# Attention and a two-layer network on one core: zero products ahead of the first chunk, another order of the first loads, and chunk 1's preparation between ticks

## The chip, the cores and the metric

The kernel runs on one core of a Trainium2 chip. A core has a matrix engine (TensorE, PE in the profile, with its weight loads shown as PEld), a vector engine (VectorE, DVE), a scalar engine (ScalarE, ACT), a general engine (GpSimd, POOL) and a synchronising engine (SyncE, SP). Each runs its own instructions in program order. Sixteen DMA engines move data between HBM and the on-chip memory (SBUF); the accumulation memory (PSUM) has eight banks, which PE writes and DVE and ACT read. The metric is the device time of one execution in microseconds, the median of several runs.

## The reference

For 4 batches, 8 heads, 768 tokens and head size 64 it computes causal attention. Heads 0, 2 and 6 see all earlier tokens. The other five heads see the first 4 tokens ("sinks") and the last 64. The output of all heads is put side by side (3072 tokens of 512 numbers) and goes through two products with a leaky ReLU between:

```
scores = scale * (q @ k.T), masked        # mask by head: causal, or causal and (sink or window)
x = softmax(scores) @ v                   # (4, 8, 768, 64) -> (3072, 512)
h = x @ w_in                              # (3072, 512) @ (512, 2048)
out = max(0.01 * h, h) @ w_out            # (3072, 2048) @ (2048, 512)
```

## The kernel before

**Tiling.** The 3072 tokens are cut into 8 chunks of 384: chunk n is half c = n % 2 of batch n // 2. For a chunk four stages follow one another: preparation (q and k transposed, so that the head dimension lies on the partitions), attention, product 1 and product 2. Heads go in pairs: pair p holds heads 2p and 2p+1.

**Stages as lists of functions.** The order of all instructions is written out by hand. A stage is a list of small functions ("slots"), and `merge` (L489 and on) deals one list evenly between the elements of another.

- `prep_first` (L227) prepares chunk 0: PE transposes k and q into PSUM, DVE and ACT copy them to SBUF.
- `prep_pair` (L193 to L214) prepares one pair of chunk 1 or 2: six PE transposes (three of k, then three of q, each of 128 tokens) into one PSUM bank, two DVE copies of k (L206) and, by ACT, one copy of q (L208).
- `prep_dma` (L216) prepares the later chunks with six transposing DMAs from SP's queue (L223 and L225); `v_shift` (L172) moves v by 64 tokens with two DMAs.
- `Attention.slots`: slot t computes the scores of unit t on PE and their exponential on ACT (L334, L370, and L312 for the sinks), DVE applies a mask where one is needed, and the product with v of unit t-LAG follows (L296). A full head has two units in an even chunk and five in an odd one, a window head has one, and the sinks of all heads are one. After a pair's last unit `finish` (L390 and on) divides by the sums on DVE (`linv` L400, `xs` L402), and three slots later `x_t` transposes the result back on PE (L411) and ACT copies it to `xt` (L412).
- `in_slots` (product 1): 16 ticks of four matmuls, 384 columns each (L457), each followed by ACT's leaky ReLU into `g` (L459). Ticks 4i to 4i+3 use quarter i of `w_in`.
- `out_slots` (product 2): three tiles of 128 tokens, 16 matmuls of 512 columns each (L470), cut into parts of 2 to 4 matmuls. After a tile's last part DVE copies it out of PSUM (L475), and SP stores it.

**PSUM.** The banks are named by tag: `ph`, `psS` and `po` have two each, `py` and `pt` one each. A new use of a tag waits until the last reader of the bank before it is done. Ticks 0 to 11 of chunk 0's product 1 take `ph` and `psS` in turn; chunk 1's scores take `psS`; the preparation of chunk 1 takes `py` and `pt` in turn.

**Loads.** Nearly all loads are issued by POOL, each as three or six pieces or one, and they pass through one software DMA queue in the order of their issue. Eight of its DMAs can be under way: each waits for the one eight places before it. The order at the start is: q of chunk 0, the identity, v of chunk 0 (`va`, three pieces; `vb`, two), all masks (`masks`, L142 to L151), quarters 0 to 2 of `w_in`, then k, q and v of chunk 1, quarter 3 of `w_in`, `w_out`, chunk 2. k of chunk 0 comes by SP's queue.

**Order around the change (L507 to L561).** Loads and constants, `prep_first`, attention of chunk 0 (`a0`, with LAG 4), ticks 0 to 11 of chunk 0's product 1 (`in0`), then the four pairs of chunk 1 in the order 0, 1, 3, 2 with the first three slots of its attention (`a1`) between them, slots 3 to 7, the last four ticks dealt among slots 8 to 15, and the first eight parts of product 2 (`out0`) dealt among the other slots of `a1`. From chunk 2 on a loop overlaps product 1 of chunk n, product 2 of chunk n-1 and attention of chunk n+1.

Of the kernel before, what the change touches and what calls it, by code (L numbers as in the profile page):

```python
# [11 lines left out]
FP32 = mybir.dt.float32  # L12
# [5 lines left out]
CH = 384  # L18
# [3 lines left out]
def kernel(  # L22
# [12 lines left out]
    nc = tc.nc  # L35
# [106 lines left out]
    def masks():  # L142
        nc.gpsimd.memset(m_caus[:], 1.0)
        keep(m_caus[:], [[1, 128]], ALU.is_ge, 0, -1)
        nc.gpsimd.memset(m_w[:], 1.0)
# [70 lines left out]
    def prep_dma(n):  # L216
        b, c = divmod(n, 2)
        i = b % 2
        qts[n] = rot.tile([128, 4, CH], BF16, name="qt", tag="qt", bufs=2)
        for g in range(3):  # L220
            t = slice(128 * g, 128 * g + 128)
            tk = slice(CH * c + 128 * g, CH * c + 128 * g + 128)
            nc.sync.dma_start_transpose(out=kt[i].rearrange("p a e t -> p (a e) t")[:, :, tk],  # L223
                                        in_=kz[n % 2][:, g].rearrange("p h d -> p (h d)"))
            nc.sync.dma_start_transpose(out=qts[n][:, :, t], in_=cast["q", n][:, g].rearrange("p h d -> p (h d)"))  # L225

    def prep_first():  # L227
# [48 lines left out]
    class Attention:  # L276
# [131 lines left out]
        def x_t(self, p, xs, tag="pt"):  # L408
            pt = bank(tag, [128, 2, 4, 128], BF16)
            for j in range(3):  # L410
                nc.tensor.transpose(pt[:, 0, j, :], xs[:, j], ident[:])  # L411
            nc.scalar.activation(out=xts[self.n][:, p, :], in_=pt[:, 0, 0:3, :], func=ACTF.Copy)  # L412
# [95 lines left out]
    make_identity(nc, ident)  # L508
    nc.vector.memset(sv[:], 0.0)
# [17 lines left out]
    for i in range(4):  # L527
# [3 lines left out]
                   x_tags=("pt", "ph", "psS", "pt")).slots(order=[0, 2, 1, 3, 4, 5, 6, 7], LAG=4, XLAG=3, sink_after={0, 2})  # L531
    run(a0[0:4])
# [35 lines left out]
    for n in range(2, NCH):  # L568
# [3 lines left out]
        if n + 2 < NCH:  # L572
            prep_dma(n + 2)
            v_shift(n + 2, nc.sync)
# [47 lines left out]
```

The softmax here doesn't subtract the row's maximum and nothing guards it: scores larger than these inputs give would overflow.

## Time and profile before

| what | value |
|---|---|
| median of 6 runs | 246.38 us (244.63 to 246.98) |
| the profiled execution's own time | 245.31 us |
| its span, first to last instruction | 243.6 us |
| PE busy | 224.5 us, 92% |
| ACT busy | 131.9 us, 54% |
| DVE busy | 90.3 us, 37% |
| POOL busy | 80.3 us, 33% |
| read from HBM, written | 27.81 MB, 6.29 MB |
| share of the closing chain: PE, DMA, DVE, ACT, POOL | 72%, 13%, 5%, 3%, 3% |

A row of a timeline gives start, duration, engine, line, operation, output and inputs with their shape, how often it stands in a row, and in brackets the engine's idle time just before it with what ended that. Ends of matmuls are modelled and stand some 0.2 us behind the last column, so the distance between starts tells the pace. A row of stretches gives, for each engine, the busy time and the number of instructions, then the clock that the throttle granted, the load of the DMA engines and GB/s. The clock column reads 1.00 also where the trace has no record of it: the first record begins 15.6 us into the span.

### The profile page before, as it was taken

The page shows a single profiled execution, that of the slowest core. Times are in us where ns is not written, and L with a number is a line of the kernel's source. Part 1 is how long each engine was busy: PE and PEld are TensorE (multiplying, and loading weights), DVE is VectorE, ACT ScalarE, POOL GpSimd, SP SyncE. Part 2 cuts the span into 40 slices and gives each one's busy share as a digit, 9 for nine tenths or more (in the row PEclk, how much of TensorE's full clock was granted, in tenths as well). Part 3 has the DMA queues.
Part 4 walks back from the last instruction along what each step waited for, and adds up shares of the span by engine and source line. Part 5 has one row for each costly group of instructions (what it writes and reads, how often), then busy time and mean ns, then how long its engine had stood idle before and what let it go on. Part 6 is the DMA issues. An engine that isn't in the chain of part 4 may idle for free.

```text
span 243.6 us, 4966 instructions
## 1 busy us (share of the span) xinstructions
PE 224.5 (92%) x1957; PEld 137.0 (56%) x1984; DVE 90.3 (37%) x257; ACT 131.9 (54%) x284; POOL 80.3 (33%) x108
## 2 busy tenths in 40 slices
PE   1788879899999999799999999999999999999994
PEld 0475546556665577465655666566556665555553
DVE  6787332706545234324421343234411342111121
ACT  2585688434663598656536665456446764333300
POOL 8994742679309961496260000000000000000000
PEclk9999999999999999999999999999999999999999
DMA  8999999999999999999999921477210111111012
GB/s 159 143 153 182 163 236 205 159 180 152 130 177 217 182 169 115 183 168 169 173 180 169 194 57 59 82 119 180 78 58 4 61 35 59 43 43 46 39 47 86
DMA packets 114858, 30.78 MB, mean 126 GB/s; under 512 B 105620, under 2 KB 110996, under 8 KB 114836
## 3 DMA queue, kind: packets, MB, share of 16 engines
q0 software_dynamic: 78304, 13.51, 77.9%
q1 hardware_dynamic: 36432, 16.95, 34.6%
q8 instruction: 15, 0.25, 0.4%
q14 instruction: 7, 0.06, 0.1%
q10 hardware_dynamic: 100, 0.02, 0.1%
HBM read 27.81 MB, written 6.29 MB: 140 GB/s over the span
## 4 chain that ended last, share of the span: by engine, by line
PE 72%; DMA 13%; DVE 5%; ACT 3%; POOL 3%; issue 1%; SPq 1%; ACTq 0%
PE ph L457 26%; PE py L470 19%; PE pt L470 6%; PE po L296 5%; PE psS L329 5%; DMA qb<-in_q_dram 4%; PE psS L470 4%; DMA qt<-qb 3%; DMA xt<-xs 3%; PE psS L365 2%; DMA f<-in_k_dram 2%; POOL kz L86 2%; DVE o L475 2%; PE psS L457 2%; PE ph L470 1%
## 5 line engine op out<-in xcount | busy, mean ns | idle before, releaser
L457 PE MATMUL ph<-xt,w_in_bf 128*128 128x384 bf16 x488 | 99.2, 326 | 0.2
L459 ACT ACTIVATE g<-ph 128x384 bf16<-128x384 f32 x122 | 60.0, 492 | 57.3 <-PE ph L457 56.6
L470 PE MATMUL py<-w_out_bf,g 128*128 128x512 bf16 (+1 forms) x238 | 63.0, 372 | 1.5
L457 PEld LDWEIGHTS <-w_in_bf 128*128 128x128 bf16 x512 | 46.0, 97 | 29.9 <-issue 0.3
L470 PEld LDWEIGHTS <-g 128*128 128x128 bf16 x400 | 36.0, 97 | 28.4 <-issue 1.4
L334 ACT ACTIVATE at<-psS 128x384 bf16<-128x384 f32 x81 | 38.8, 491 | 13.4 <-PE psS L329 11.6
L329 PE MATMUL psS<-qt,kt 128*128 128x384 bf16 (+2 forms) x104 | 26.6, 296 | 3.3 <-ACT at L334 1.2
L93 POOL DMA_DIRECT2D qb<-in_q_dram x24 | 21.4, 912 | 21.9 <-DMA qt<-qb 9.9
L475 DVE COPY o<-py 128x512 f32<-128x512 f32 (+1 forms) x16 | 10.8, 674 | 45.3 <-PE py L470 45.3
L86 POOL DMA_DIRECT2D kz<-in_k_dram x30 | 22.5, 777 | 14.7 <-DMA kt<-kz 12.8
L93 POOL DMA_DIRECT2D va<-in_v_dram x24 | 21.3, 914 | 6.6 <-DMA w_out_bf<-in_moe_w_out_dram 3.3
L370 ACT ACTIVATE ats<-psS 128x384 bf16<-128x384 f32 x38 | 18.5, 492 | 4.9 <-PE psS L365 4.4
L296 PE MATMUL po<-va,at 128*128 128x65 bf16 x237 | 20.4, 196 | 0.3 <-DVE at L338 0.3
L296 PEld LDWEIGHTS <-at 128*128 128x128 bf16 x252 | 16.4, 100 | 7.6 <-DVE at L338 1.2
L402 DVE TENSOR_TENSOR xs<-po,linv 128x384 bf16<-128x384 f32 x30 | 16.7, 557 | 1.0
L329 PEld LDWEIGHTS <-kt 128*128 128x128 bf16 x108 | 10.7, 101 | 10.5 <-issue 3.3
L340 DVE TENSOR_TENSOR at<-at,m_caus 128x128 bf16<-128x128 bf16 x24 | 5.4, 224 | 30.2 <-ACT at L334 30.1
L470 PE MATMUL pt<-w_out_bf,g 128*128 128x512 bf16 x57 | 15.7, 379 | 0.4
L365 PEld LDWEIGHTS <-kt 128*128 128x128 bf16 x240 | 12.4, 101 | 5.2 <-issue 0.2
L296 PEld LDWEIGHTS <-ats 128*128 128x128 bf16 x240 | 11.9, 99 | 3.8 <-DVE xs L402 0.3
L365 PE MATMUL psS<-qt,kt 128*128 128x64 bf16 x228 | 13.1, 195 | 0.0
L338 DVE TENSOR_TENSOR at<-at,m_caus 128x256 bf16<-128x256 bf16 x24 | 7.0, 292 | 15.8 <-ACT at L334 15.5
(102 smaller groups left out, 189.3 us busy)
## 6 DMA issues: line engine op xcount, KB each, us to landing
out_dram<-o SPq DMA_DIRECT2D x23, 256.0 KB, 3.0
qb<-in_q_dram POOLq DMA_DIRECT2D x24, 128.0 KB, 6.3
va<-in_v_dram POOLq DMA_DIRECT2D x24, 128.0 KB, 7.3
w_in_bf<-in_moe_w_in_dram POOLq DMA_DIRECT2D x4, 512.0 KB, 7.7
w_out_bf<-in_moe_w_out_dram POOLq DMA_DIRECT2D x4, 512.0 KB, 13.7
kz<-in_k_dram POOLq DMA_DIRECT2D x30, 64.0 KB, 6.5
vb<-va SPq DMA_DIRECT2D x8, 195.0 KB, 7.4
vb<-va SPq DMA_DIRECT2D x6, 130.0 KB, 5.0
```

The costliest lines, as they stand in the source:

```text
L86: nc.gpsimd.dma_start(out=kz[n % 2][:, g, hh::2, D * hh : D * hh + D], in_=nat[nm][b, c, :, hh::2, g])
L93: nc.gpsimd.dma_start(out=o, in_=nat[nm][b, c, :, :, g])
L296: nc.tensor.matmul(o, lhsT=lhsT, rhs=rhs, start=first, stop=False, skip_group_check=True)
L329: nc.tensor.matmul(s[:, off : off + w], lhsT=kt[i][:, p, hh, 128 * kj : 128 * kj + 128], rhs=qts[n][:, p, lo:CH], start=(j == 0), stop=(j ...
L334: nc.scalar.activation(out=a[:, 0:off], in_=s[:, 0:off], func=ACTF.Exp, scale=SM)
L365: nc.tensor.matmul(s[:, 64 * m : 64 * m + 64], lhsT=kt[i][:, p, hh, k0 : k0 + 128], rhs=qts[n][:, p, 64 * m : 64 * m + 64], start=(m == 0) ...
L370: nc.scalar.activation(out=av_, in_=s[:, 0:CH].rearrange("p (j e f) -> p j e f", j=3, e=2), func=ACTF.Exp, scale=SM)
L402: nc.vector.tensor_tensor(xs[:], po[:, :, :, 0:D], linv.to_broadcast([128, 3, 2, D]), op=ALU.mult)
L457: nc.tensor.matmul(ph[:, 0:CH], lhsT=w_in_bf[:, g, 128 * t : 128 * t + 128], rhs=xts[n][:, g, :], start=(g == 0), stop=(g == KG - 1))
L459: nc.scalar.activation(out=gs[n][:, t, :], in_=ph[:, 0:CH], func=ACTF.Prelu, alpha=0.01)
L470: nc.tensor.matmul(py[n][:, 0 : c1 - c0], lhsT=gs[n][:, ng, 128 * tt : 128 * tt + 128], rhs=w_out_bf[:, ng, c0:c1], start=(ng == 0), stop= ...
L475: nc.vector.tensor_copy(o[:, 0 : c1 - c0], py[n][:, 0 : c1 - c0])
```

## The change

Five edits, all at or before the start of chunk 2:

1. `warm_up(n, w)` issues n matmuls of zeros, w columns wide, into a `psS` bank that nothing reads. It is called with 9 of 512 columns at the start, with 9 of 128 ahead of the second half of k in `prep_first`, with 8 ahead of q's first piece and 2 ahead of each later one, and with 12 ahead of chunk 0's attention. Its first call puts a memset of 128x512 on DVE. In chunk 0, `x_t` issues 6, 4, 6 and 10 transposes of the identity (by pair) ahead of its own three.
2. `masks` is cut in two. The causal mask (`mask_causal`) now stands ahead of v's loads on POOL, the other two masks stand between quarter 0 and quarter 1 of `w_in`.
3. Nine ticks of product 1 stand ahead of chunk 1's preparation, not twelve; ticks 9, 10 and 11 follow its first, second and third pair.
4. The list of slots that is dealt among the first eight parts of product 2 has six empty slots at its end, not four.
5. `prep_dma` returns its seven steps as a list, which its callers run at once; the steps and their order are the same.

```diff
-    def masks():
+    def mask_causal():
         nc.gpsimd.memset(m_caus[:], 1.0)
         keep(m_caus[:], [[1, 128]], ALU.is_ge, 0, -1)
+
+    def masks():
         nc.gpsimd.memset(m_w[:], 1.0)
...
+    idle = {}
+
+    def warm_up(n, w=128):
+        if not idle:
+            idle["s"] = bf("idle", 512)
+            nc.vector.memset(idle["s"][:], 0.0)
+            idle["d"] = bank("psS", [128, 512], FP32)
+        for _ in range(n):
+            nc.tensor.matmul(idle["d"][:, 0:w], lhsT=idle["s"][:, 0:128], rhs=idle["s"][:, 0:w], start=True, stop=True)
...
             if nm == "q":
                 continue
+            if half == 1:
+                warm_up(9)
             for e in range(2):
...
+        warm_up(8)
         for g in range(3):
+            warm_up(2 if g else 0)
             for p in range(4):
...
         def x_t(self, p, xs, tag="pt"):
             pt = bank(tag, [128, 2, 4, 128], BF16)
+            for j in range((6, 4, 6, 10)[p] if self.n == 0 else 0):
+                nc.tensor.transpose(pt[:, 1, j % 4, :], ident[:], ident[:])
             for j in range(3):
...
     load(0, "q")
     make_identity(nc, ident)
+    warm_up(9, 512)
     nc.vector.memset(sv[:], 0.0)
...
+    mask_causal()
     load(0, "v")
     load_vb0()
+    load_w("in", 0)
     masks()
-    for i in range(3):
-        load_w("in", i)
+    load_w("in", 1)
+    load_w("in", 2)
     load(1)
...
+    warm_up(12)
     run(a0[0:4])
...
-    run(in0[0:12])
+    run(in0[0:9])
 
     for j, p in enumerate((0, 1, 3, 2)):
         prep_pair(1, p, ("py", "pt")[j % 2], "vva")
+        run(in0[9 + j : 10 + j] if j < 3 else [])
         if j == 1:
...
-    run(merge(out0[0:8], a1[16:] + [lambda: None] * 4))
+    run(merge(out0[0:8], a1[16:] + [lambda: None] * 6))
     v_shift(2, nc.sync)
     load(4)
-    prep_dma(3)
-    v_shift(3, nc.sync)
+    run(prep_dma(3))
```

More of the change, by code (lines that the diff above doesn't have):

```diff
@@ L219, in prep_dma, with k_step, q_step @@
         qts[n] = rot.tile([128, 4, CH], BF16, name="qt", tag="qt", bufs=2)
-        for g in range(3):
+        def k_step(g):
+            t = slice(CH * c + 128 * g, CH * c + 128 * g + 128)
+            nc.sync.dma_start_transpose(out=kt[i].rearrange("p a e t -> p (a e) t")[:, :, t],
+                                        in_=kz[n % 2][:, g].rearrange("p h d -> p (h d)"))
+        def q_step(g):
             t = slice(128 * g, 128 * g + 128)
-            tk = slice(CH * c + 128 * g, CH * c + 128 * g + 128)
-            nc.sync.dma_start_transpose(out=kt[i].rearrange("p a e t -> p (a e) t")[:, :, tk],
-                                        in_=kz[n % 2][:, g].rearrange("p h d -> p (h d)"))
             nc.sync.dma_start_transpose(out=qts[n][:, :, t], in_=cast["q", n][:, g].rearrange("p h d -> p (h d)"))
+        return [lambda f=f, g=g: f(g) for g in range(3) for f in (k_step, q_step)] + [lambda: v_shift(n, nc.sync)]
     def prep_first():
@@ L572 @@
         if n + 2 < NCH:
-            prep_dma(n + 2)
-            v_shift(n + 2, nc.sync)
+            run(prep_dma(n + 2))
         if n + 1 < NCH:
```

## The prediction

> **What bounds the kernel now.** First I read the page's busy shares (PE 92%), then the stretches: from 50 to 98 us PE is busy 47.7 of 48 us. A microsecond is therefore won only where PE waits, and the waits lie in five places: before 20 us, at 28.5 to 36, at 45 to 49, at 98 to 104, and in small pieces later. For each I ask which wait ends last. PE's timeline of the first 21 us shows the pace:
>
> ```profile
> 10.51 0.53 PE L329 MATMUL psS<-qt,kt 128*128 128x256 bf16 x2
> 10.83 0.53 PE L329 MATMUL ph<-qt,kt 128*128 128x384 bf16 x1
> 19.72 0.34 PE L411 MATMUL pt<-ident,xs 128*128 128x128 bf16 x3 [0.88 <-DVE xs L402]
> 20.80 0.81 PE L457 MATMUL psS<-xt,w_in_bf 128*128 128x384 bf16 x4
> 21.45 0.81 PE L457 MATMUL ph<-xt,w_in_bf 128*128 128x384 bf16 x4
> ```
>
> 384 columns take 0.32 us at 10.5, but 0.65 / 4 = 0.162 us at 20.8: the first rows run at half pace. Starts 0.03 us apart for 65 columns appear first at 15.6. So PE is slow until then, and in 16 to 20 us it waits for the chain of DVE and ACT.
>
> What comes after is set by loads. POOL's timeline, then the load of the DMA engines by stretches (last two columns: mean load, GB/s), then the landing of chunk 1's last q piece:
>
> ```profile
> 9.56 0.27 POOL L143 MEMSET m_caus<- 128x128 bf16 x1
> 10.16 0.17 POOL L145 MEMSET m_w<- 128x64 bf16 x1
> 11.54 2.27 POOL L99 DMA_DIRECT2D w_in_bf<-in_moe_w_in_dram  x3
> 16.38 2.69 POOL L93 DMA_DIRECT2D qb<-in_q_dram  x3
> ...
> 4.50:12.00 7.50, 5.04 (x33) 3.48 (x34) 5.59 (x14) 3.70 (x7) 7.11 (x15) 1.00 2.19 150
> 12.00:14.00 2.00, 2.00 (x34) 1.88 (x33) 1.37 (x11) 1.72 (x5) 2.00 (x4) 1.00 0.63 39
> 14.00:21.00 7.00, 5.16 (x80) 3.90 (x78) 5.74 (x18) 4.33 (x10) 5.95 (x7) 1.00 1.24 205
> ...
> DMA to landing us min/median/max: 10.2/10.2/10.2
> ```
>
> The last q piece is issued at 18.1 and lands 10.2 us later, at 28.3. The queue is full from 14 us on; between 12 and 14 it moves 39 GB/s instead of 150, a hole of (150 - 39) / 150 x 2 = 1.5 us, because POOL makes masks before it issues the first weights. PE meets the landing exactly:
>
> ```profile
> 27.95 0.33 PE L201 MATMUL py<-ident,kb 128*128 128x128 bf16 x3
> 28.12 0.48 PE L201 MATMUL py<-ident,qb 128*128 128x128 bf16 x3
> 29.99 0.32 PE L329 MATMUL psS<-qt,kt 128*128 128x384 bf16 x1 [1.06 <-ACT qt L208]
> 32.43 0.32 PE L329 MATMUL psS<-qt,kt 128*128 128x384 bf16 x1 [0.89 <-ACT at L334]
> 33.20 0.33 PE L329 MATMUL psS<-qt,kt 128*128 128x256 bf16 x2 [0.35 <-ACT at L334]
> ...
> 32.65 3.70 ACT L334 ACTIVATE at<-psS 128x384 bf16<-128x384 f32 x8
> ```
>
> The q row takes 0.48 instead of 0.33: its third transpose waited for that piece. Then copies bound: DVE's k copies, ACT's q copies, and from 32.65 eight exponentials without a break.
>
> **1. Zero products: nothing.** The nine wide ones start when DVE's memset is done, near 1.3 us, and fill the wait before 5.43 at some 0.43 us each (512 columns at 0.32 per 384). The memset costs as the 128x256 f32 one, 0.27, on a DVE that is busy until its first cast at 4.75. The 9, 8, 4 and 12 narrow ones, at 0.11 each if slow (six transposes take 0.82, of which 0.2 is the modelled end) or 0.055, add up to 3.6 or 1.8 us in waits of 0.5 to 0.9; at worst some 1 us reaches the path. The 26 extra transposes, 0.2 to 0.6 us per pair, stand in waits of 0.4 to 1.05. Against that, scores at full pace let ACT run its 12 exponentials 0.38 apart (10.76, 11.14, 11.52 show that) instead of over 5.8 us: 1.2 us at most. The last `vb` piece lands at 8.70 + 5.2 = 13.9, and part 2 makes that 14.5, about when the first window head uses it (14.59); I take 0.5 of gain. All of it, -1.2 to +1, is hidden: nine ticks end at 19.9 + 9 x 0.65 + 0.25 = 26.0, and q lands at 27.2 (part 2). Were that cover gone, the 0.5 would count.
>
> The Trainium skill ("TensorE: Matmul & The Clock Gate", Part 1) says that PE starts at half clock and needs about 3.4 us of steady work for the full one. The trace agrees with the two paces; by the rule alone half of the 5.3 us from 10.24 to 15.6 would be won, and the sum below would be -2.8 instead of -0.1. The q landing speaks against booking it.
>
> **2. POOL's order: -1.1 us at q's landing.** The causal mask's memset and selection (9.56 to 10.16, 0.6 us) move ahead of v's five loads, so these issue and land up to 0.6 later. The first weights no longer wait for the other masks (10.16 to 11.54), so they are issued 1.38 earlier, less little. The queue gains the smaller of 1.34 and the hole less 0.6, 0.9 to 1.1 (the hole is 1.5 by the rates, 1.7 if its edges are read at 12.2 and 13.9). I take 1.1, since the first weight bytes move about 2.3 us after the issue, so 10.2 + 2.3 = 12.5 falls inside v's last bytes (12.8). Bounds 0 (another hole opens between first and second weights) and 1.34. The later masks delay the second quarter by nothing: it is issued at 12.3 as before, and its turn comes at 15. The window mask is ready at about 11.8, and DVE takes it up at 12.64. Everything behind in the full queue, to 56 us, lands 1.1 earlier: q of chunk 1 at 27.2, the last quarter of `w_in` and `w_out` too, where nobody waits. Quarter 2 is there before tick 8.
>
> **3. Ticks 9 to 11 between the pairs: +1.0.** Twelve matmuls of 0.162 (1.95 us of PE) and three ReLUs of 0.49 move behind q's landing, into the stretch where PE waits 1.06 + 0.89 + 0.35. PE has room; ACT and the `psS` banks have not. I count from the end of pair 0's transposes (28.60 before), with 0.72 per pair on DVE, 0.49 on ACT (0.38 when full), 0.34 per pair and 0.65 per tick on PE; before in brackets, from ACT's and DVE's rows:
> - k copy of the second pair 1.04 (0.79): its transposes stand behind tick 9.
> - its q copy 1.86 (1.61); then tick 10's ReLU, so the first exponential 2.63 (1.99).
> - slot 1's scores need the bank that slot 0's exponential frees, and wait on PE until 3.1, because ticks 9 and 11 take `psS` banks as well.
> - pair 2's transposes stand behind them on PE: k copy 3.90 (2.84), q copy 4.72 (3.66), third exponential 5.11 (4.05).
>
> From there ACT is full (3.70 us for eight), so the 1.06 stays; I book 1.0. Lowest 0, if the ReLUs fit in ACT's gaps (0.81, 0.27, 0.43: 1.5 us against three times 0.49); highest 1.5, all three ReLUs added. With part 2 the last four ticks start as before, near 35.7.
>
> **4. Two more empty slots: +0.5.** Slots of `a1` move ahead by one against the parts of product 2. Before, the last two `x_t` lie between the fifth part and the sixth and cover the copy of `py`:
>
> ```profile
> 46.21 1.67 PE L470 MATMUL py<-w_out_bf,g 128*128 128x512 bf16 x7
> 47.72 0.33 PE L411 MATMUL pt<-ident,xs 128*128 128x128 bf16 x3
> 48.63 0.33 PE L411 MATMUL pt<-ident,xs 128*128 128x128 bf16 x3 [0.58 <-DVE o L475]
> 48.79 1.46 PE L470 MATMUL py<-w_out_bf,g 128*128 128x512 bf16 x6
> ```
>
> After, both come ahead of the fifth part. They still wait 0.75 for each other's `pt` bank (ACT's copy), and the sixth part then waits for the copy uncovered: 0.2 + 0.69 + 0.05 = 0.95. Of the waits of 41.8 to 45.8 (some 1.2 us) the earlier scores fill about 0.45. Net 0.5, from 0 to 0.95.
>
> **5. Later: -0.5.** One more wait is for a DMA:
>
> ```profile
> 103.53 0.32 PE L329 MATMUL psS<-qt,kt 128*128 128x384 bf16 x1 [0.84 <-DMA qt<-qb]
> ```
>
> SP's transposes for it begin at 83.94, when the store before them is out, which PE paces; one of them takes 5.04 us to issue while chunk 5's loads are in the queue. Those loads come 1.1 earlier, PE 0.4 later, so they overlap less. The wait can fall to nothing (-1.0 with its neighbours' share) or stay; I take the middle. `prep_dma`'s list is the same instructions: 0.
>
> **Sum:** 0 - 1.1 + 1.0 + 0.5 - 0.5 = -0.1. The profiled execution (span 243.6, 1.7 outside) took 245.31, so 245.2 by it; it stands 1.07 below the median, so against the median 246.3.
>
> **Rivals.** What can be told from no change here is about 0.5%, 1.2 us.
> - *The ticks really fill the waits (faster).* If ReLUs and banks fit, part 3 is 0; with the whole wait at 103 gone: -1.1 + 0 + 0.5 - 1.0 = -1.6, 244.8. For it: PE idles 2.3 us there, ACT 1.5. Against: the bank order above.
> - *Chunk 1's loads land when they did (slower).* If q still lands at 28.3, because v's delay opens a hole as long as the one closed, PE waits longer ahead of pair 0 and parts 3 and 4 count whole: 0 + 1.0 + 0.5 = +1.5, 247.9. It decides as soon as the landing moves by less than 0.3. For it: v's first piece lands 4.8 us after its issue, hardly queued. Against: the queue moved 150 GB/s without a break from 4.5 to 12.
> - *The clock falls back in the new wait of 26.0 to 27.2.* Then 3.4 us at half pace would add 1.7: 248.0. Against: waits of 1.05 and 1.2 us passed without it.
> - *The zero products don't raise the pace at all.* The time is then the forecast's, since part 1 counts nothing.
>
> **Chances.** Forecast 0.46, and 0.04 for the last rival with it: 0.50 within 0.5%. Faster 0.28. Loads unmoved 0.18 and clock 0.04: 0.22 slower. The range reaches to the faster and the slower case, with -1.8 from part 2's 1.34, part 4's half cost and the wait at 103: 244.5 to 248.0. The likeliest alone: 245.2 to 247.4.
>
> **What would show it.** Right: full pace from about 5 to 9 us on; no hole at 12 to 14; chunk 1's q transposes near 27.2 with PE waiting over 1 us before them; ticks 9 to 11 within 27.5 to 30, the third exponential near 32.7; the sixth part of product 2 about 0.95 after the fifth. Wrong: q landing at 28 or later, a third exponential before 32, an unchanged or longer wait at 103, or half pace after 16 us.

## The result and the profile after

| | before | changed |
|---|---|---|
| median, all runs | 245.47 us (69 runs) | 247.08 us (32 runs) |
| ratio | | 1.0063, 95% interval 1.0045 to 1.0081 |
| the profiled execution | 245.31 us, span 243.6 | 249.63 us, span 247.9 |

The changed kernel is slower by 0.63%, some 1.55 us; the forecast was no change. The ratio is taken from the fast executions alone: six of the changed kernel's 33, counting the profiled one, which is among them, are more than 1.5% above its fastest and are left out. So its profile shows an execution 2.5 us above the median, with a fall of PE's clock that costs about 1 us; the profile of the kernel before shows one without a fall. Most executions of both kernels have one, as is counted below (after_kept), so this 1 us belongs to the pair of profiles and not to the change.

First the page of the changed kernel: busy time, the granted clock in 40 slices of 6.2 us, and the closing chain by engine.

```profile
PE 230.8 (93%) x2025; PEld 139.5 (56%) x2052; DVE 89.9 (36%) x258; ACT 131.2 (53%) x284; POOL 80.3 (32%) x108
...
PEclk9999889999999999999999999999999999999999
...
PE 67%; DMA 22%; POOL 4%; DVE 2%; ACT 2%; issue 2%; SPq 0%; ACTq 0%; POOLq 0%
```

The share of DMA in the closing chain grew from 13% to 22%, and the clock shows a dent in the fifth and sixth slice, 25 to 37 us. PE's timeline of the changed kernel up to the landing of chunk 1's q:

```profile
1.26 4.02 PE L180 MATMUL psS<-idle 128*128 128x512 bf16 x9 [1.26 <-DVE idle L177]
...
9.93 0.32 PE L352 MATMUL ph<-qt,kt 128*128 128x384 bf16 x1
...
10.26 0.33 PE L352 MATMUL ph<-qt,kt 128*128 128x384 bf16 x1
...
18.75 0.34 PE L436 MATMUL pt<-ident,xs 128*128 128x128 bf16 x3 [0.32 <-DVE xs L425]
19.39 0.82 PE L482 MATMUL ph<-xt,w_in_bf 128*128 128x384 bf16 x4 [0.30 <-DMA w_in_bf<-in_moe_w_in_dram]
...
24.60 0.81 PE L482 MATMUL ph<-xt,w_in_bf 128*128 128x384 bf16 x4
25.25 0.22 PE L214 MATMUL py<-ident,kb 128*128 128x128 bf16 x1
...
27.52 0.23 PE L214 MATMUL py<-ident,qb 128*128 128x128 bf16 x1 [0.73 <-DMA qb<-in_q_dram]
28.51 0.23 PE L214 MATMUL py<-ident,qb 128*128 128x128 bf16 x1 [0.75 <-DMA qb<-in_q_dram]
29.50 0.29 PE L214 MATMUL py<-ident,qb 128*128 128x128 bf16 x1 [0.76 <-DMA qb<-in_q_dram]
29.58 1.49 PE L482 MATMUL psS<-xt,w_in_bf 128*128 128x384 bf16 x4
30.86 0.53 PE L214 MATMUL pt<-ident,kb 128*128 128x128 bf16 x3
```

Between 9.93 and 10.26 lies one more row of scores, so these rows start 0.165 us apart, where they started some 0.3 apart before: the zeros do raise the pace, and product 1 starts at 19.39 instead of 19.90. But PE is then done with nine ticks at 25.25 and stands before chunk 1's pieces until 29.50, with six lone transposes in 4.3 us. The last q piece lands there 1.1 us later than before (28.3), not 1.1 earlier. At 29.58 four matmuls take 1.28 from start to next start, twice the 0.65 of 24.60: the clock has fallen.

POOL's timeline of the changed kernel, the issues of these loads:

```profile
9.85 0.80 POOL L99 DMA_DIRECT2D w_in_bf<-in_moe_w_in_dram  x1
...
12.25 1.51 POOL L99 DMA_DIRECT2D w_in_bf<-in_moe_w_in_dram  x2
...
19.63 0.88 POOL L93 DMA_DIRECT2D qb<-in_q_dram  x1 [1.49 <-DMA w_in_bf<-in_moe_w_in_dram]
```

The same time by stretches (last two columns: load of the DMA engines, GB/s):

```profile
12.00:14.00 2.00, 1.30 (x30) 0.96 (x30) 1.93 (x12) 2.00 (x6) 2.00 (x4) 1.00 1.46 172
14.00:17.00 3.00, 2.90 (x62) 2.56 (x61) 2.90 (x11) 1.82 (x5) 3.00 (x4) 1.00 1.11 156
17.00:21.00 4.00, 3.27 (x38) 2.14 (x36) 2.67 (x7) 1.76 (x5) 2.02 (x3) 1.00 1.27 203
```

And the time from issue to landing of the first weight quarter:

```profile
DMA to landing us min/median/max: 9.5/9.5/9.5
```

The first weights are issued at 9.85 instead of 11.54, and the hole at 12 to 14 is closed (172 GB/s against 39). But from 14 to 17 the queue moves 156 where it moved 203, the first quarter needs 9.5 us to land instead of 5.4, and the last q piece, which waits for the DMA eight places before it, that quarter, is issued at 19.63 instead of 18.1.

ACT's timeline of the changed kernel, with the third exponential of chunk 1, from which ACT is full:

```profile
35.38 0.49 ACT L221 ACTIVATE qt<-pt 128x384 bf16<-128x384 bf16 x1
35.77 3.69 ACT L357 ACTIVATE at<-psS 128x384 bf16<-128x384 f32 x8
```

And PE's, around product 2's fifth part and at two later waits:

```profile
49.40 0.33 PE L436 MATMUL pt<-ident,xs 128*128 128x128 bf16 x3
50.31 0.33 PE L436 MATMUL pt<-ident,xs 128*128 128x128 bf16 x3 [0.58 <-ACT xt L437]
50.47 1.02 PE L495 MATMUL py<-w_out_bf,g 128*128 128x512 bf16 x4
52.28 1.89 PE L495 MATMUL py<-w_out_bf,g 128*128 128x512 bf16 x8 [0.78 <-DVE o L500]
...
106.62 0.32 PE L352 MATMUL psS<-qt,kt 128*128 128x384 bf16 x1 [0.44 <-DMA qt<-qb]
...
133.92 0.32 PE L482 MATMUL ph<-xt,w_in_bf 128*128 128x384 bf16 x1 [1.32 <-DMA xt<-xs]
```

The span's 4.3 us more are made up so: landing of q +1.1 (29.45 against 28.32); third exponential 6.32 after the landing against 4.33, of which 1.0 are the ticks and 1.0 the half pace (parted below); from product 1's last tick (43.05; before 39.94) to the sixth part of product 2 (52.28; before 48.79) 9.23 against 8.85, +0.4; waits for transposing DMAs later +0.8 (the one for `qt` fell from 0.84 to 0.44, one for `xt` grew from 0.14 to 1.32). 1.1 + 2.0 + 0.4 + 0.8 = 4.3.

### The profile page after: what moved, and what is told of

Same layout as the page of the kernel before. It is cut to its first block, busy times and chain, and to the rows that moved or that the text cites. A ratio compares the mean times of both kernels' runs of the same rounds, so it can differ in the third digit from the quotient of the medians.

```text
span 247.9 us, 5101 instructions
## 1 busy us (share of the span) xinstructions
PE 230.8 (93%) x2025; PEld 139.5 (56%) x2052; DVE 89.9 (36%) x258; ACT 131.2 (53%) x284; POOL 80.3 (32%) x108
## 4 chain that ended last, share of the span: by engine, by line
PE 67%; DMA 22%; POOL 4%; DVE 2%; ACT 2%; issue 2%; SPq 0%; ACTq 0%; POOLq 0%
PE ph L482 24%; PE py L495 18%; DMA qb<-in_q_dram 7%; PE pt L495 5%; PE po L319 5%; PE psS L352 4%; DMA w_in_bf<-in_moe_w_in_dram 4%; PE psS L495 3%; DMA xt<-xs 3%; DMA qt<-qb 3%; DMA va<-in_v_dram 3%; PE psS L388 2%; DVE o L500 2%; POOL qb L93 1%; PE ph L495 1%
## 5 line engine op out<-in xcount | busy, mean ns | idle before, releaser
L352 PE MATMUL psS<-qt,kt 128*128 128x384 bf16 (+2 forms) x104 | 26.0, 290 | 1.6 <-ACT g L484 0.6
L352 PEld LDWEIGHTS <-kt 128*128 128x128 bf16 x108 | 10.4, 98 | 10.7 <-issue 3.4
L388 PEld LDWEIGHTS <-kt 128*128 128x128 bf16 x240 | 11.7, 98 | 5.5 <-issue 0.6
```

What stands on the lines that cost most here:

```text
L352: nc.tensor.matmul(s[:, off : off + w], lhsT=kt[i][:, p, hh, 128 * kj : 128 * kj + 128], rhs=qts[n][:, p, lo:CH], start=(j == 0), stop=(j ...
L388: nc.tensor.matmul(s[:, 64 * m : 64 * m + 64], lhsT=kt[i][:, p, hh, k0 : k0 + 128], rhs=qts[n][:, p, 64 * m : 64 * m + 64], start=(m == 0) ...
```

## The experiments

Two theories stand against each other. The forecast's: POOL's order brings q 1.1 us earlier and so pays for ticks and slots. The rival's: chunk 1's loads land no earlier, and ticks (+1.0) and slots (+0.5) count whole. A third, the clock's fall, was taken up with the second group. Ratios are to the kernel before on the same chip, with 95% intervals.

What the profiles of all kernels show at the disputed places, in us from the start of the span (one execution each, the ratio from all; both profiles of the changed kernel, changed and after_look, are of executions of 249.6 and 249.1 us against a median of 247.1):

| kernel | first weights issued, landed | last q piece lands | third exponential | difference | ratio |
|---|---|---|---|---|---|
| before | 11.54, 16.92 | 28.32 | 32.65 | 4.33 | 1 |
| changed | 9.85, 19.35 | 29.45 | 35.77 | 6.32 | 1.0063 |
| only_queue | 10.07, 17.21 | 28.13 | 32.46 | 4.33 | 1.0033 |
| only_ticks | 11.54, 16.98 | 28.51 | 33.84 | 5.33 | 1.0026 |
| only_slots | 11.52, 16.90 | 28.61 | 32.94 | 4.33 | 1.0009 |
| only_zeros | 10.94, 16.54 | 28.32 | 33.03 | 4.71 | 1.0028 |
| no_queue | 10.95, 16.31 | 28.40 | 33.73 | 5.33 | 1.0063 |
| no_ticks | 9.84, 18.12 | 29.07 | 33.40 | 4.33 | 1.0071 |
| no_zeros | 10.09, 18.31 | 29.62 | 37.22 | 7.60 | 1.0076 |
| after_kept | 9.86, 17.12 | 28.38 | 33.72 | 5.34 | 1.0048 |
| only_causal | 11.54, 17.06 | 28.27 | 32.59 | 4.32 | 0.9982 |
| only_w0 | 9.57, 17.36 | 28.03 | 32.35 | 4.32 | 0.9999 |
| kept_before | 11.53, 17.05 | 28.59 | 32.92 | 4.33 | 0.9998 |
| early_q | 11.54, 17.0 | 25.48 | 29.81 | 4.33 | 0.9953 |
| causal_back | 9.00, 16.88 | 28.74 | 34.06 | 5.32 | 1.0012 |
| after_look | 9.86, 17.65 | 29.89 | 36.67 | 6.78 | - |
| queue_look | 10.07, 17.88 | 28.54 | 32.86 | 4.32 | - |
| early_q_causal | 11.52, 17.08 | 25.48 | 30.48 | 5.00 | 0.9927 |

### Each part alone

**only_queue**: part 2 on the kernel before.

```diff
+    mask_causal()
     load(0, "v")
     load_vb0()
+    load_w("in", 0)
     masks()
-    for i in range(3):
-        load_w("in", i)
+    load_w("in", 1)
+    load_w("in", 2)
```

> The kernel before with POOL's new order alone (causal mask ahead of v's loads, first weights ahead of the other two masks). Theory A (the new order delays the loads: in the changed kernel's trace the first weights landed at 19.35 instead of 16.92 and chunk 1's last q piece at 29.45 instead of 28.3): q again lands near 29.4, PE waits for it after its twelve ticks, and the time rises by about 1.1 us (ratio 1.0045). Theory B (the order is harmless, the ticks and the wait do the damage): q lands at 27.2 to 28.3 and the time moves by less than 0.3 us (ratio 0.999 to 1.001).

Measured: 1.0033 (1.0006 to 1.0059), slower if anything. q lands at 28.13 instead of 28.32: 0.2 us of the 1.1. The rival holds on the landing; that the order alone costs time at all is not in either theory. The profile can't show where: its execution took 243.87 us, the fastest of the twelve, whose median is 246.67.

**only_ticks**: part 3 on the kernel before.

```diff
-    run(in0[0:12])
+    run(in0[0:9])
...
         prep_pair(1, p, ("py", "pt")[j % 2], "vva")
+        run(in0[9 + j : 10 + j] if j < 3 else [])
```

> The kernel before with ticks 9 to 11 of product 1 moved between chunk 1's pairs, nothing else. q lands at 28.3 as before; PE has nine ticks ahead of it and reaches it at 26.0, so it waits some 2.3 us. Theory B (the ticks behind the landing delay the third exponential by 1.0 us, and the longer wait can let the clock fall): the time rises by 1.0 us (ratio 1.004), and more in executions where the pace halves after the wait. Theory A (the loads do it): the ticks fill PE's waits and the time moves by less than 0.3 us.

Measured: 1.0026 (0.9993 to 1.0058), +0.6 us with an interval that reaches to no change. The profile is sharper. ACT's timeline of this kernel:

```profile
30.63 0.49 ACT L208 ACTIVATE qt<-pt 128x384 bf16<-128x384 bf16 x1
31.02 0.48 ACT L459 ACTIVATE g<-ph 128x384 bf16<-128x384 f32 x1
31.39 0.50 ACT L334 ACTIVATE at<-psS 128x384 bf16<-128x384 f32 x1
...
33.84 3.69 ACT L334 ACTIVATE at<-psS 128x384 bf16<-128x384 f32 x8
```

The ReLU of a tick stands between copy and exponential, and the third exponential comes 5.33 after the landing instead of 4.33. The table has 5.32 to 5.34 in every kernel with the ticks whose pace is full there, and 4.32 to 4.33 in those without them whose PE isn't late for another reason (only_zeros and early_q_causal have other waits ahead).

**only_slots**: part 4 on the kernel before.

```diff
-    run(merge(out0[0:8], a1[16:] + [lambda: None] * 4))
+    run(merge(out0[0:8], a1[16:] + [lambda: None] * 6))
```

> The kernel before with six empty slots instead of four, nothing else. The prediction's part 4 expects the sixth part of product 2 to start about 0.95 us after the fifth ends, the last two transposes of the attention ahead of the fifth, and +0.5 us in all (ratio 1.002). The rival: the earlier scores fill the waits and the time does not move (0.999 to 1.001).

Measured: 1.0009 (0.9983 to 1.0035): too small to be told from nothing. PE's timeline of this kernel has the forecast's wait:

```profile
48.97 0.33 PE L411 MATMUL pt<-ident,xs 128*128 128x128 bf16 x3 [0.58 <-ACT xt L412]
49.13 1.03 PE L470 MATMUL py<-w_out_bf,g 128*128 128x512 bf16 x4
50.94 2.10 PE L470 MATMUL py<-w_out_bf,g 128*128 128x512 bf16 x9 [0.78 <-DVE o L475]
```

From the last tick (41.71) to 50.94 are 9.23 us, as in the changed kernel, against 8.85 before: +0.38 net.

**only_zeros**: all `warm_up` calls, the extra transposes in `x_t` and the list in `prep_dma`, nothing else.

```diff
+    warm_up(9, 512)
...
+            if half == 1:
+                warm_up(9)
...
+        warm_up(8)
...
+            for j in range((6, 4, 6, 10)[p] if self.n == 0 else 0):
+                nc.tensor.transpose(pt[:, 1, j % 4, :], ident[:], ident[:])
```

> The kernel before with the zero products and the identity transposes alone. Both theories expect full pace from some 5 to 9 us on, chunk 0's attention done 0.5 to 1.2 us earlier, and the time unchanged (ratio 0.999 to 1.001), because PE then waits for chunk 1's q at 28.3 instead. If the wait of about 1 us ahead of q is enough to halve the pace, or if the zeros delay the first preparation, the time rises by 0.5 us or more; if the q landing does not bound, it falls by 0.5 to 1.2.

Measured: 1.0028 (1.0003 to 1.0052). In its profile the full clock is granted from 10.0 us, later than in the changed kernel's (5.2): until then the narrow zeros cost twice as much and stand ahead of chunk 0's transposes. Attention of chunk 0 begins at 11.42 instead of 10.24 and product 1 at 20.43 instead of 19.90. So the zeros can cost, by 0.5 us on PE's path here. One difference stands ahead of it: DVE's first cast of k takes 0.98 us here (5.03 to 6.01), while POOL issues v's loads from 4.61 on, and 0.62 in the changed kernel, whose v loads begin at 5.48, behind the causal mask. no_queue and causal_back, which also have zeros and the causal mask behind v, show 0.98 and 0.99 and a full clock from 10.64 and 10.29; the four profiles with zeros and the causal mask ahead of v have it from 4.69 to 6.74. So the place of the causal mask, a part of part 2, goes with the early clock in all seven.

The four ratios above one add up to 0.96%, the whole change has 0.63%.

### Each part taken out of the changed kernel

**no_queue**, **no_ticks**, **no_zeros** undo part 2, part 3 and part 1 in the changed kernel: the diffs above with the signs turned.

> The changed kernel with POOL's old order (all masks behind v's loads, then three quarters of the weights); zeros, ticks and slots stay. Theory A (POOL's new order costs: alone it gave ratio 1.0033): the last q piece of chunk 1 lands at 28.3 to 28.6 instead of 29.45, and the time falls from 1.0063 to about 1.003. Theory B (the ticks and the bare wait ahead of q cost, whatever the order): PE waits from about 25.5 to 28.4, the third exponential comes near 33.8, and the ratio stays between 1.005 and 1.007.

> The changed kernel with all twelve ticks ahead of chunk 1's preparation; zeros, POOL's order and slots stay. Theory B: PE is busy until about 27.2, waits 1 to 2 us for q and not 4, and the time falls by 1.0 us or more (ratio about 1.002), more where the pace no longer halves after the wait. Theory A: the landing decides, the third exponential comes as late as before the edit, and the ratio stays at 1.005 or more.

> The changed kernel without the zero products and the identity transposes; POOL's order, ticks and slots stay. Theory C (the zeros cost: where the pace is still half, they stand ahead of chunk 0's transposes, and chunk 0's attention starts at 11.4 instead of 10.24, as in the run of the zeros alone, ratio 1.0028): the ratio falls to about 1.0035. Rival (with nine ticks ahead, PE waits for q in any case, so the zeros change nothing): it stays at 1.005 to 1.007.

Measured: no_queue 1.0063 (1.0034 to 1.0091), no_ticks 1.0071 (1.0039 to 1.0102), no_zeros 1.0076 (1.0039 to 1.0113). No part is the cause by itself. Without the new queue the time is the same 1.0063: part 2 is worth nothing in sum, and zeros, ticks and slots cost 1.55 us without it, against the rival's 1.5. That no_ticks is not faster contradicts a simple sum: by the table it wins 1.0 at the third exponential. Its executions nearly all carry a fall of the clock (11 of 12 by their mean granted clock); its profiled one does not and took 246.43 us. Among executions with a fall it is 0.6 us faster than the changed kernel (247.4 against 248.0), so part of what it wins is lost because it falls more often. Why it does is open.

**after_kept**: the changed kernel with eight zero products ahead of each transpose of chunk 1's first pair, so that PE isn't bare while q comes.

```diff
+                if n == 1 and p == 0:
+                    warm_up(8)
                 nc.tensor.transpose(pt[:, e, g, :], cast[nm, n][:, g, 2 * p : 2 * p + 2, :], ident[:])
```

> The changed kernel with eight more zero products (128 columns) ahead of each of the six transposes of chunk 1's first pair, so that PE is not bare while it waits for k and q. They compute nothing. Theory B's second half (the clock falls because PE is bare for 3 to 4 us): the clock's records show no stretch of 3.4 us at half pace from 26 to 33, and the median falls by about 1 us (ratio about 1.002 to 1.003). Rival (the fall of the clock is no larger part of the loss than before the change): the ratio stays at 1.005 to 1.007; or the zeros themselves delay the transposes and it rises.

Measured: 1.0048 (1.0017 to 1.0078). PE's timeline of this kernel:

```profile
28.01 0.61 PE L180 MATMUL psS<-idle 128*128 128x128 bf16 x8
28.46 0.22 PE L216 MATMUL py<-ident,qb 128*128 128x128 bf16 x1
28.51 0.81 PE L484 MATMUL psS<-xt,w_in_bf 128*128 128x384 bf16 x4
29.16 0.33 PE L216 MATMUL pt<-ident,kb 128*128 128x128 bf16 x3
```

Ticks after the landing are at full pace (0.65 to the next row), and the third exponential is back at 5.34. All 12 executions keep the full clock, against 12 of 33 of the changed kernel. (A fall of 3.41 us to half takes 0.007 from the mean granted clock of a span of 245 us. Means of 0.997 to 0.999 hold none: in the profiles of after_kept, 0.998, and only_zeros, 0.997, the clock is half only from 243.62 and 242.15 on, at the end of the span.) With the fall gone 0.48% remains.

The same count for other kernels (causal_back is described further down), with the kernel before as it ran beside them on four chips:

| kernel | executions without a fall, median | with a fall, median |
|---|---|---|
| before | 34 of 125, 244.5 | 91, 245.8 |
| changed | 12 of 33, 246.5 | 21, 248.0 |
| no_queue | 11 of 12, 247.0 | 1, 247.5 |
| no_ticks | 1 of 12, 246.4 | 11, 247.4 |
| no_zeros | 3 of 12, 245.9 | 9, 248.1 |
| after_kept | 12 of 12, 246.2 | none |
| causal_back | 9 of 12, 245.5 | 3, 247.2 |

The kernel before has falls too, and not more seldom: 73% of its executions against 64%. With the fall or without, the changed kernel is some 2 us slower, so the fall doesn't make the difference between the two. It does blur the ratios of kernels that fall more or less often: without a fall no_queue is 0.5 us slower than the changed kernel, though the ratios are the same, and after_kept is some 1.4 slower than the kernel before on its chip (244.8 without a fall). Where the kernel before falls no profile of it shows. In only_slots and in only_w0 (further down), whose ticks and scores stand as in the kernel before, the clock is half from 35.45 to 38.86 and from 34.86 to 38.27, and the last tick comes 8.77 us after the third exponential instead of 7.29: the fall costs 1.48 there. The first of the last four ticks in only_slots and in the kernel before:

```profile
36.24 1.47 PE L457 MATMUL ph<-xt,w_in_bf 128*128 128x384 bf16 x4
...
35.75 0.81 PE L457 MATMUL ph<-xt,w_in_bf 128*128 128x384 bf16 x4
```

**kept_before**: the kernel before, with such fillings in its own waits (the extra transposes of chunk 0's `x_t`; 16, 12 and five times 4 zero products between chunk 1's slots).

```diff
         if j > 0:
+            warm_up((0, 16, 0, 12)[j])
             run(a1[j - 1 : j])
...
-    run(a1[3:8])
+    for s_ in a1[3:8]:
+        warm_up(4)
+        run([s_])
```

> The kernel before with the identity transposes ahead of chunk 0's x_t and with zero products (128 columns, into a ph bank) in PE's waits of chunk 1's first eight slots: 16 ahead of slot 0, 12 ahead of slot 2, 4 ahead of each of slots 3 to 7. Nothing is issued before chunk 0's attention and no load is moved; the products compute nothing. Theory (a fall of the clock in these waits is what separates executions of one kernel: those of the kernel before at full clock have a median of 244.6, the others 245.4 to 246.0): most executions keep the full clock, and the median falls by 0.6 to 0.9 us (ratio about 0.997). Rival (the difference goes with the clock but not by it): the clock stays full and the time does not move, ratio 0.999 to 1.002.

Measured: 0.9998 (0.9971 to 1.0024), though all 12 executions kept the full clock, against 12 of 35 of the kernel before beside it. That one takes 244.3 without a fall and 245.9 with one, kept_before 245.5: by these medians the fillings cost most of what the kept clock saves.

### The two halves of POOL's order, and another order

**only_causal**: the causal mask ahead of v's loads, all weights behind the other masks. **only_w0**: the first weights ahead of all masks, v where it was. Both on the kernel before.

```diff
+    mask_causal()        # only_causal
     load(0, "v")
     load_vb0()
+    load_w("in", 0)      # only_w0
     masks()
```

> The kernel before with the causal mask alone ahead of v's loads; the other masks and the three quarters of the weights keep their order. In the runs so far the first weights landed at 16.3 to 17.0 and chunk 1's last q piece at 28.3 to 28.6 in the old order, and at 17.1 to 19.4 and 28.1 to 29.6 in the new one, with packets of 0.5 to 1.3 us between 14 and 17 us only in the new one. If delaying v by 0.3 to 0.6 us is what makes the first weights slow, this run shows such packets, the weights near 18 and q at 28.8 or later, and the time rises by 0.5 us (ratio 1.002). If the early issue of the first quarter is, this run is like the kernel before: q at 28.3 to 28.6, ratio 0.999 to 1.001.

> The kernel before with the first quarter of the weights issued ahead of all masks, near 9.6 us; v is not delayed. If the early issue of a lone quarter makes its packets slow (an issue of 9.8 to 10.1 landed after 7.1 to 9.5 us, one of 11.5 after 5.4), this run shows slow packets at 13 to 16 us again, and q lands at 28.3 or later although the queue has no hole: ratio 1.000 to 1.003. If v's delay is what does it, the hole closes cleanly, the weights land near 15.5 and q near 27.2, and the time moves by less than 0.3 us, since PE arrives at 28.

Measured: 0.9982 (0.9951 to 1.0013) and 0.9999 (0.9967 to 1.0031), with q at 28.27 and 28.03. Neither half shows a cost by itself, and neither brings q by more than 0.3.

**early_q**: k and q of chunk 1 ahead of the third weight quarter. The ticks that use this quarter go among chunk 1's slots, and take `ph` banks only.

```diff
-    for i in range(3):
-        load_w("in", i)
-    load(1)
+    load_w("in", 0)
+    load_w("in", 1)
+    load(1, "kq")
+    load_w("in", 2)
+    load(1, "v")
...
-    run(in0[0:12])
+    run(in0[0:8])
...
-    run(a1[3:8])
+    run(merge(in0[8:12], a1[3:8]))
```

> The kernel before with k and q of chunk 1 ahead of the third quarter of w_in in the queue, chunk 1's first three slots right after its pairs as before, and ticks 8 to 11 dealt among slots 3 to 7 (their bank always ph). If the landing of chunk 1's q is what ends last there, q lands near 25.9 instead of 28.4, the third exponential comes near 30.3 instead of 32.65, the four ticks then cost some 1.3 to 1.8 us on ACT, and the time falls by 0.5 to 1.0 us (ratio 0.996 to 0.998). Rival (ACT bounds the whole stretch to 36 us, wherever it starts): the ticks take back all of it, ratio 0.999 to 1.003.

Measured: 0.9953 (0.9920 to 0.9987), faster than both kernels. q lands at 25.48 and the third exponential comes at 29.81, 2.8 earlier. In the time 1.2 of that is left.

**causal_back**: the changed kernel with the causal mask behind v again, the first weights still ahead of all masks. **after_look** and **queue_look**: the changed kernel and only_queue profiled once more. **early_q_causal**: early_q with the causal mask ahead of v.

```diff
-    mask_causal()
     load(0, "v")
     load_vb0()
     load_w("in", 0)
+    mask_causal()
     masks()
```

> The changed kernel with one thing undone: the causal mask is made behind v's loads again, together with the other masks; the first weights stay ahead of all masks. So v is not delayed. Theory A (v's delay is what makes the weights' packets slow): the first weight quarter lands at about 17.4 as with the weights moved alone, chunk 1's last q piece at 28.0, and the time is 1.0 us under the changed kernel's, ratio to before 1.002 to 1.004. Theory B (the landing differs from execution to execution and v has nothing to do with it): q lands anywhere from 28.0 to 29.6 and the ratio stays at 1.005 to 1.008.

> The changed kernel, profiled a second time. Theory A (its queue order always delays the weights): the first quarter lands at 18.1 or later and chunk 1's last q piece at 29 or later, as in its first profile (19.35 and 29.45). Theory B (the landing differs from execution to execution): the first quarter lands near 17.2 and q near 28.2, as in the profile of the queue order alone.

> The kernel before with POOL's new order alone, profiled a second time. Theory A (what else the changed kernel does, its zeros and ticks, is needed for slow weights): first quarter at 17.2, q at 28.1 as in its first profile. Theory B (the landing differs from execution to execution): either can come, first quarter 17 to 19.4, q 28 to 29.6. In no case does q land at 27.2, as the prediction had it.

> The kernel before with k and q of chunk 1 loaded ahead of the third weight quarter and ticks 8 to 11 dealt among chunk 1's slots, and the causal mask made ahead of v's loads. If the two gains add (0.9953 and 0.9982 alone): 0.9935, some 243.9 us. If the causal mask's place was worth nothing: 0.995, 244.4, with q of chunk 1 at 25.5 in both.

Measured: causal_back 1.0012 (0.9983 to 1.0040), below the changed kernel's interval. after_look lands q at 29.89, queue_look at 28.54. The stretches of causal_back:

```profile
12.00:14.00 2.00, 1.91 (x38) 1.59 (x36) 1.17 (x5) 2.00 (x6) 2.00 (x3) 1.00 1.37 175
14.00:17.00 3.00, 2.31 (x46) 1.62 (x46) 2.89 (x16) 2.70 (x7) 3.00 (x5) 1.00 1.23 202
```

and PE's timeline of it before the landing:

```profile
26.00 0.81 PE L482 MATMUL ph<-xt,w_in_bf 128*128 128x384 bf16 x4
26.65 0.33 PE L214 MATMUL py<-ident,kb 128*128 128x128 bf16 x3
26.83 0.23 PE L214 MATMUL py<-ident,qb 128*128 128x128 bf16 x1
27.86 0.23 PE L214 MATMUL py<-ident,qb 128*128 128x128 bf16 x1 [0.80 <-DMA qb<-in_q_dram]
28.78 0.23 PE L214 MATMUL py<-ident,qb 128*128 128x128 bf16 x1 [0.69 <-DMA qb<-in_q_dram]
28.85 0.81 PE L482 MATMUL psS<-xt,w_in_bf 128*128 128x384 bf16 x4
```

With v back, the queue runs at 202 from 14 to 17. All seven profiles that have v late and the first weights early lie below that there (146 to 195: changed 156, after_look 170, no_ticks 146, no_zeros 176, only_queue 187, queue_look 162, after_kept 195); those with one of the two alone don't (only_w0 200, only_causal 198, causal_back 202), though after_kept's 195 is hardly below them. So the slow stretch takes v's delay, as theory A has it, and the early weights with it. But theory A is wrong on the landing: q still comes at 28.74, not 28.0; on the time it is right. What changed on PE in the profiles is the other side of the wait: the full clock comes at 10.29 instead of 5.18, chunk 0 is done 1.4 later (last early tick at 26.0 instead of 24.6), the wait before the landing is 2.0 us long instead of 4.3, the profiled clock doesn't fall, and 9 of 12 executions keep it. That this makes the time is not shown: the profiled execution took 246.92 us, the slowest of those nine, and its third exponential (34.06) is later than that of no_queue (33.73), whose time is longer.

In the changed kernel the two halves of part 2 thus have opposite signs: the first weights' place 1.0063 to 1.0012 (no_queue against causal_back), the causal mask's place back up to 1.0063. The first of these two steps has intervals that touch (1.0034 to 1.0040), so its size is uncertain.

That a landing doesn't follow the queue's rate can be read from what the DMA engines had moved by then. The stretch from the start to q's landing, kernel before:

```profile
0.00:28.32 28.32, 19.51 (x188) 13.69 (x188) 19.28 (x58) 16.59 (x32) 22.91 (x38) 1.00 1.61 159
```

and changed:

```profile
0.00:29.45 29.45, 22.55 (x244) 14.42 (x244) 19.56 (x59) 14.85 (x29) 23.04 (x38) 0.99 1.67 162
```

28.32 us at 159 GB/s are 4.50 MB, 29.45 at 162 are 4.77: when q's last bytes arrive, the queue has moved 0.27 MB more than it had before, 1.7 us of its time at 155 to 160. In only_w0 it is 28.03 at 166, 4.65 MB. The bytes were brought forward, and later pieces passed q's last bytes. The trace shows how: it keeps sixteen completion records for each load, as many as there are DMA engines, and the landing is the last of them. The eighth and the sixteenth:

| kernel | first weights, 8th and 16th | last q piece, 8th and 16th |
|---|---|---|
| before | 16.74, 16.92 | 27.35, 28.32 |
| only_w0 | 15.37, 17.36 | 25.99, 28.03 |
| no_queue | 16.08, 16.31 | 26.71, 28.40 |
| causal_back | 15.07, 16.88 | 25.56, 28.74 |
| changed | 15.50, 19.35 | 26.66, 29.45 |
| early_q | 16.71, 17.00 | 24.74, 25.48 |

In only_w0 the first weights are issued 2 us earlier, ahead of all masks, and nothing else is moved: eight of the sixteen parts of q's piece are complete 1.36 earlier, the last 0.29. From no_queue to causal_back, which differ in the place of the first weights alone, the eighth record moves by -1.15 and the sixteenth by +0.34. In the changed kernel thirteen of the first quarter's sixteen records stand by 15.91, the last at 19.35. So the gain arrives in the middle of the sixteen and not in the last one. Which engine is last, and why, the records don't tell.

early_q_causal: 0.9927 (0.9899 to 0.9955), 243.99 us: the lowest median here. The product of early_q and only_causal (0.9935) lies in its interval, but so does the 0.995 expected if the causal mask's place is worth nothing, so the sum of the two gains isn't shown. POOL's timeline of this kernel:

```profile
13.01 2.66 POOL L93 DMA_DIRECT2D kb<-in_k_dram  x3
15.62 2.68 POOL L93 DMA_DIRECT2D qb<-in_q_dram  x3
18.21 0.84 POOL L99 DMA_DIRECT2D w_in_bf<-in_moe_w_in_dram  x1
```

and PE's:

```profile
25.28 0.81 PE L459 MATMUL psS<-xt,w_in_bf 128*128 128x384 bf16 x4
25.93 0.33 PE L203 MATMUL py<-ident,kb 128*128 128x128 bf16 x3
26.10 0.33 PE L203 MATMUL py<-ident,qb 128*128 128x128 bf16 x3
```

q is issued ahead of the third quarter and has landed (25.48) when PE comes to it (25.93), so PE doesn't wait for a DMA there at all.

## Why the prediction was wrong, step by step

The forecast was -0.1 us and the runs show +1.55. The outcome is the rival "chunk 1's loads land when they did", priced at +1.5. That its number fits so well is partly luck: among executions with a fall, and among those without, the difference is some 2 us, and the zeros and later waits, which it had at 0, have a share in it.

- **Part 1, zero products: booked 0, cover named.** In the changed kernel it held: they raised the pace from 5 us on, and what chunk 0 won (product 1 at 19.39 instead of 19.90) went into the wait for q. As a term by itself it was too kind: alone they cost 0.28%, and in that profile the pace is full only from 10.0 us. Parts 1 and 2 hang together: the early clock came only where the causal mask stands ahead of v.
- **Part 2, POOL's order: booked -1.1 at q's landing. This is the step that failed.** The hole closed as forecast. But the step took the whole piece to move with the queue's mean rate, and the landing is the last of sixteen records. Where the first weights alone are moved, the eighth record of q's piece does come forward about as booked, by 1.36 (only_w0) and 1.15 (causal_back against no_queue), and the sixteenth moves by -0.29 and +0.34. In the seven profiles with both halves the eighth is only 0.1 to 0.8 earlier than before, and the landing 0.2 earlier (only_queue) to 1.6 later (after_look); it lies nowhere below 28.0 while q keeps its place in the queue. The stated reason of the rival, a new hole as long as the old, is not what happened either: the weights move at 146 to 195 GB/s from 14 to 17 us, and their last parts land late. The step also took all issues behind the first quarter as unmoved, and in the changed kernel's profile POOL waits 1.49 for that quarter before it can issue the last q piece. That isn't the cause: in after_look the piece is issued at 17.93 without a wait and lands last of all, at 29.89.
- **Part 3, ticks between pairs: booked +1.0.** 1.0 at the third exponential in every pair of profiles at full pace. As time of the whole kernel it is less certain: +0.6 alone (interval to 0), and no gain when taken out of the changed kernel (0.6 among executions with a fall).
- **Part 4, two more empty slots: booked +0.5.** +0.38 on PE's path, by the copy that is no longer covered (0.78 on the row, 0.95 forecast with what surrounds it). The time of only_slots can't resolve it.
- **Part 5, the wait near 103: booked -0.5.** The wait for `qt` fell by 0.4 (0.84 to 0.44 on the row). But the next one for a transposing DMA, near 133, is 1.32 instead of 0.14 in this profile. Over the kernels run here the first lies between 0 and 0.84 and the second between 0 and 1.65, in both orders of POOL, so neither can be put down to the change.
- **Rival "the clock falls back", given 0.04.** Falls are common, 21 of 33 executions with 1.5 us between the medians, but it isn't the cause: the kernel before has them in 91 of 125. The reason against it ("waits of 1.05 and 1.2 us passed without it") was read from one execution that happened to have none. In the three profiles that fall ahead of q (changed, after_look, no_zeros) the wait was 3.9 to 5.1 us long, as the landing didn't come.

The signs named in advance came out so: full pace from 5 us, yes; no hole at 12 to 14, yes; q's transposes near 27.2, no, 29.5; ticks 9 to 11 within 27.5 to 30, no, 29.6 to 33.1; third exponential near 32.7, no, 35.8; sixth part about 0.95 after the fifth, yes. "q landing at 28 or later" and "half pace after 16 us" were the named signs of a wrong forecast, and both are there.

Open: why packets slow down when v is late and the first weights early, which DMA engine lags and why, why causal_back is faster than no_queue, and why no_ticks, which falls more often, isn't faster.

## What to carry to other kernels

A hole in a DMA queue is worth what it brings forward at the landing that somebody waits for, and that has to be read from the landings of the pieces, which the last of their sixteen parts sets, not from the rate; to bring one load earlier, move it ahead of another load in the queue (early_q: 2.8 us) rather than tighten what stands before both. Work moved behind such a landing counts whole if the landing doesn't move, so price it without the gain as well. When the work ahead gets faster and the load it meets does not, only the wait grows. And before a fall of the clock in one profile is made a cause, count how often the kernel before has one: here 91 of 125 against 21 of 33.

## What the runs showed of the hardware

- The granted clock changes on a grid of 3.41 us whose place differs from execution to execution. In the changed kernel it is full from 5.18 to 29.08 (23.9 us, seven times 3.41) and half to 32.49 (one time); in after_look full for 20.48 us (six) and half for 6.83 (two); in no_zeros half for 6.83; in early_q_causal full for 6.83, half for 3.41. The Trainium skill ("TensorE: Matmul & The Clock Gate", Part 1) has a free-running window of about 3.4 us after which the clock is set by the activity in it, and says that the number of slow matmuls therefore differs from run to run; these records agree. Its Part 4 adds that transposes don't count as activity in the same way, and the wait that lost the clock here held nothing else; no run here tells them from idle time.
- What a fall costs depends on where it lies. In only_ticks it lies at 19.14 to 22.55, ahead of the wait for q, and the third exponential is 5.33 after the landing as without a fall; in only_slots, at 35.45 to 38.86, it costs 1.48 us.
- The same zeros brought the full clock at 4.7 to 6.7 us in the profiles where PE's pause before k's transposes was 0.4 to 0.65, and at 10.0 to 10.6 in the three where it was 0.8 (only_zeros, no_queue, causal_back). The longer pause goes with a longer cast of k on DVE (0.98 against 0.62). The grid's place may do it as well as the pause.
- The landing of one and the same load, chunk 1's last q piece, lies between 28.1 and 29.9 in kernels with the same queue order. Its sixteen completion records spread over 1.2 us (before) to 3.5 (changed). The gap between two pieces of q is 0.8 to 1.1 as a rule and was 1.5 in two profiles (no_queue 26.90 to 28.40, after_kept 26.83 to 28.38).
